# Start addresses of the streamed operands moved off multiples of 64 bytes in a two-mixture float32 block

## The chip, the cores and the metric

The kernel runs on one core of a Trainium2 chip. The time is device microseconds (us) of that core for one execution of the whole program. Durations of single instructions are in nanoseconds (ns).

## The reference, cut to what matters

An attention with a sigmoid in place of a softmax is followed by two dense feed-forward layers, called mixtures here. All arrays are float32.

```
scores = q @ k.T / sqrt(64) - log(448);  attn = sigmoid(scores);  o = attn @ v     # 4 batches x 12 heads x 448 x 64
x = o as [1792 tokens, 768]
h = x @ w_in;  x = (h * cos(h)) @ w_out                                           # 768 -> 2048 -> 768
g = x @ w_gate;  v = x @ w_val;  out = (g * sigmoid(g) * v) @ w_out               # 768 -> 1536 -> 768
```

## The kernel before, in words

Everything is held transposed: features lie on the 128 partitions, tokens along the free dimension, in four groups of 448 tokens. One matmul takes a 128x128 block of weights as the stationary operand and streams 448 columns of tokens past it, as the moving operand.

The precision of float32 is got from pairs. A value is split into a high part `hi` (a copy in float32r, the format that TensorE streams in one pass) and a low part `lo` (the rest, `value - hi`). A product is three matmuls, in the order of `THREE`: hi by hi, hi by lo, lo by hi. Each of them has its own weight load.

The stages:

- Attention, over 24 pairs of heads. Line 655 makes scores, line 667 and line 691 the remainder of 64 keys, line 687 weighs the values, with plain float32 operands. The result is split into the tile of the first mixture's input: hi by ScalarE (line 723), lo by VectorE (line 625).
- The first mixture. Line 1007 multiplies the input `X1` by blocks of `w_in`; ScalarE and VectorE make h*cos(h) from the result and `split_g` writes its hi and lo into one of four activation buffers `g0` to `g3`; line 867 multiplies these by blocks of `w_out`.
- The second mixture. Line 953 makes the gate and the value products by a scheme with seven products of half matrices in place of eight (tokens `1 5 2 6 7 3 4`); their moving operands are seven tiles `X[i]`, made from the sums of the first mixture, hi and lo, in the room of the first input. The activations go through the same four buffers `g0` to `g3` into line 867.

The input tiles `x0` and `x1` hold 43,008 bytes on each partition. `X1` and `X` are views of them, and `rest`, the last part of `x1`, becomes room for weight pairs in the second mixture. Each activation buffer holds hi and lo of 448 tokens, 3,584 bytes on a partition. Every operand in these tiles begins a multiple of 448 elements (1,792 bytes, which is 28 times 64) or of 384 elements (1,536 bytes, 24 times 64) from the tile's start, and each tile starts on a multiple of 64 bytes.

Which instruction comes when on each engine is set by a planner (`Order`) that runs while the program is built, with costs written in the code; a matmul costs `PRODUCT = 0.2025` us there. Nothing in the planner looks at an address. Helper lines 236 and 239 record most ScalarE and VectorE operations, so in the profile these are told apart by their tiles.

Of the kernel before, what the change touches and what calls it, by code (L numbers as in the profile page):

```python
# [10 lines left out]
F32R = mybir.dt.float32r  # L11
# [139 lines left out]
def block_kernel(  # L151
# [12 lines left out]
    P = 128  # L164
# [3 lines left out]
    KD = outT.shape[0] // P  # L168
    T = outT.shape[1]
    N = S  # L170
    KH = KD // 2
    W = KH * P
    NH = T // (2 * N)
# [13 lines left out]
    xp = ctx.enter_context(tc.tile_pool(name="xp", bufs=1))  # L187
# [5 lines left out]
    R = [xp.tile([P, 2, KD, N], F32, tag=f"r{h}", name=f"r{h}") for h in range(NH)]  # L193


    first_x = [xp.tile([P, KD * 2 * 2 * N], F32R, tag=f"x{h}", name=f"x{h}") for h in range(NH)]
    X1 = [x.rearrange("p (k m t) -> p k m t", k=KD, m=2) for x in first_x]
    PLACES = {1: (0, 0), 5: (0, 1), 2: (0, 2), 6: (0, 3), 7: (1, 0), 3: (1, 1), 4: (1, 2)}
    size = KH * 2 * N
# [21 lines left out]
    pairs, singles, gslots, tmps, downbanks = (Slots(order) for _ in range(5))  # L221

    def make_pairs(pool, n, name):
        for i in range(n):
            pairs.give(pool.tile([P, 2, 2, KH, P], F32R, tag=f"w{name}{i}", name=f"w{name}{i}"))
# [217 lines left out]
    def loads():  # L443
        for n, need in enumerate(needs()):
            if n == 2 * NF1 - 4:
                free_t.give((yield convs))
            t = yield free_t
            for w, f, i, k in need:
                there, event = scratch[id(w), f + i]
                yield event  # L450
                there = scratch[id(w), f + i][0]
                if k is None:
                    yield move(t, there)
                else:
                    yield move(t[:, i * W:(i + 1) * W], there[:, k * W:(k + 1) * W])
            arrived = order.event()
            arrivals.append((t, arrived))
            if waiting_load:
                waiting_load.pop(0).set()
            order.spawn(landed(arrived), 0)  # L460
# [101 lines left out]
    def inputs(h):  # L562

        b11, b12, b21, b22 = (R[h][:, j, k * KH:(k + 1) * KH] for k in range(2) for j in range(2))
        make = {
            1: (b11, None), 2: (b21, None), 5: (b11, (b12, b11)), 6: (b11, (b22, b11)),
            7: (b12, (b22, b12)), 4: (b21, (b21, b11)), 3: (b22, None),
        }

        def to_hi(out, t):  # L570
            def do(engine):
                if engine == "ACT":
                    nc.scalar.activation(out=out, in_=t, func=AF.Copy)
                else:
                    nc.vector.tensor_copy(out, t)  # L575
            return {"ACT": 1.55, "DVE": 1.2}, do


        made_t, split_x = ({i: order.event() for i in ORDER} for _ in range(2))
        after = {5: [split_x[1]], 6: [split_x[5]], 7: [made_t[5]], 4: [split_x[2], made_t[6]]}  # L580

        def operand_of(i):
            t, parts = make[i]
            time = due[n_first + h * (NF2 // 2), 0, i]
            if parts:
                for event in after[i]:
                    yield event
                yield by(time - 5.0, vec(1.6, t, parts[0], parts[1], SUB))
                made_t[i].set()
            yield x_left[h - 1, i] if h else x_used[PLACES[i][0]]  # L590
            hi, lo = X[i][:, :, 0], X[i][:, :, 1]
            yield by(time - 3.2, to_hi(hi, t))
            yield by(time - 1.7, vec(1.6, lo, t, f32(hi), SUB))
            split_x[i].set()
            x_ready[h, i].set()

        yield source[h]
        for i in ORDER:
            order.spawn(operand_of(i), 0)
# [419 lines left out]
    def tensor_engine():  # L1019
        turn = itertools.count()  # L1020
        downs = (want for want in ())
        for n in range(n_units):
            if n < n_first:
                for i in range(2):
                    yield from up(n, i, upbanks[next(turn) % 4])
                    for _ in range(between(n)[i]):
                        yield from some(downs)
            else:
                z = {}
                for u in range(2):  # L1030
                    yield from seven(n, u, next(turn), z, downs)
            downs = down(n)
            if n_first - 2 <= n < n_first or n == n_first + NF2 // 2 - 1:
                order.spawn(presets(n), 0)
        while (yield from some(downs)):
            pass

    with tc.manual_schedule():
        nc.gpsimd.memset(nlog, -math.log(S))
        for h in range(NH):  # L1040
            order.spawn(inputs(h), 3.5)
        order.spawn(loads(), 3)
        order.spawn(operands(), 4)
        for raw, t in lent:
            returned.append(order.event())
            order.spawn(conversions(raw, t, returned[-1]), end)
        attention()
        with tc.tile_pool(name="mp", bufs=1) as mp:
            for i in range(2):
                raws.give(mp.tile([P, WT, 2], I32, tag=f"raw{i}", name=f"raw{i}"))  # L1050
                order.spawn(conversions(), end)
            sum_room.append(mp.tile([P, W], F32, tag="sum", name="sum"))
            convs.give(mp.tile([P, WT], F32, tag="cv", name="cv"))
            convs.give(ring[:, 2])
            make_pairs(mp, 3, "b")
            for i in range(4):
                gslots.give(mp.tile([P, 2, N], F32R, tag=f"g{i}", name=f"g{i}"))
            for i in range(3):
                tmps.give(mp.tile([P, 2, N], F32, tag=f"u{i}", name=f"u{i}"))
            order.spawn(tensor_engine(), 0)  # L1060
            order.run()
            assert not order.open
# [51 lines left out]
```

## Time and profile before

| what | value |
|---|---|
| median of the runs shown (lowest, highest) | 1119.46 us (1116.98 to 1119.54) |
| span of the profiled execution, first to last instruction | 1111.8 us |
| median less that span | 7.7 us |
| TensorE matmul busy | 1099.8 us, 99% of the span |
| TensorE share of the chain that ended last | 95% |
| VectorE busy, ScalarE busy, GpSimd busy | 827.0, 578.8, 83.0 us |
| DMA queues, mean rate | 132 GB/s |

The device time of the profiled execution by itself is not listed; its span stands for it, with 7.7 us around it. Matmuls are pipelined: one matmul's record lasts about 365 ns, while the next one starts some 200 ns after it. So the pace is read from how many matmuls lie in a stretch without a gap, and not from the mean duration of one.

### The profile page before, as it was taken

How to read it: one execution, taken by the hardware profiler on the slowest of the kernel's cores; microseconds unless marked ns; L12 is line 12 of the kernel's file. 1: busy time of each engine (PE TensorE's matmuls, PEld its weight loads, DVE VectorE, ACT ScalarE, POOL GpSimd, SP SyncE). 2: the span in 40 equal slices, each digit the busy share in tenths (PEclk: the TensorE clock that was granted, in tenths of full speed). 3: DMA queues.
4: the chain of work that ended last, by engine and by line, in shares of the span. 5: the costliest groups of instructions: out<-in, count | busy, mean ns of one | idle time of the engine just before them, and what ended most of it. 6: DMA issues, size and time to landing. Idle time of an engine off the chain costs nothing.

```text
span 1111.8 us, 14428 instructions
## 1 busy us (share of the span) xinstructions
PE 1099.8 (99%) x5555; PEld 963.7 (87%) x5555; DVE 827.0 (74%) x1193; ACT 578.8 (52%) x868; POOL 83.0 (7%) x70
## 2 busy tenths in 40 slices
PE   9999999999999999999999999999999999999998
PEld 5555579999999999999999889999998999999997
DVE  6888866788788878887778977687779636546644
ACT  5877766644454444454446765444436654333330
POOL 0000000000000000000000321111212101102100
PEclk9999999999999999999999999999999999999999
DMA  7997635544454434443422244434431421121102
GB/s 220 238 252 191 164 114 178 195 153 160 131 178 146 164 117 156 156 146 112 140 101 86 94 148 160 152 128 157 143 128 54 143 88 57 43 72 57 43 1 99
DMA packets 51908, 146.42 MB, mean 132 GB/s; under 512 B 5760, under 2 KB 21120, under 8 KB 51840
## 3 DMA queue, kind: packets, MB, share of 16 engines
q1 hardware_dynamic: 51696, 145.28, 41.1%
q8 instruction: 43, 0.70, 0.3%
q10 hardware_dynamic: 144, 0.23, 0.1%
q14 instruction: 25, 0.20, 0.1%
HBM read 113.25 MB, written 32.24 MB: 131 GB/s over the span
## 4 chain that ended last, share of the span: by engine, by line
PE 95%; DVE 4%; DMA 0%; issue 0%; ACT 0%; ACTq 0%; DVEq 0%
PE banks L867 36%; PE banks L953 26%; PE banks L1007 21%; PE banks L687 5%; PE banks L655 5%; PE banks L691 2%; PE banks L667 1%; DVE x L239 1%; DVE r L239 1%; DVE u L239 1%; DMA r<-in_qk 0%; DVE g L239 0%; DVE wb L239 0%; DVE x L575 0%; ACT r L236 0%
## 5 line engine op out<-in xcount | busy, mean ns | idle before, releaser
L867 PE MATMUL banks<-g,wb 128*128 128x448 f32 x1080 | 240.2, 366 | 0.6 <-DVE g L239 0.6
L867 PEld LDWEIGHTS banks<-g,wb 128*128 128x128 f32 x1080 | 202.8, 188 | 17.5 <-DVE g L239 0.9
L239 DVE TENSOR_TENSOR r<-banks,r 128x896 f32<-128x896 f32 (+1 forms) x133 | 144.0, 1083 | 98.5 <-PE banks L867 97.2
L867 PE MATMUL banks<-g,wa 128*128 128x448 f32 x792 | 179.9, 366 | 1.5 <-DVE g L239 1.5
L867 PEld LDWEIGHTS banks<-g,wa 128*128 128x128 f32 x792 | 148.7, 188 | 13.9 <-DVE g L239 1.9
L953 PE MATMUL banks<-x,wb 128*128 128x448 f32 x702 | 152.2, 366 | 1.4 <-DVE wb L239 0.7
L953 PEld LDWEIGHTS banks<-x,wb 128*128 128x128 f32 x702 | 131.7, 188 | 12.9 <-DVE wb L239 1.1
L1007 PE MATMUL banks<-x,wb 128*128 128x448 f32 x648 | 137.2, 365 | 0.0
L1007 PEld LDWEIGHTS banks<-x,wb 128*128 128x128 f32 x648 | 121.8, 188 | 9.6
L236 ACT ACTIVATE u<-u 128x448 f32<-128x448 f32 x150 | 86.3, 576 | 73.7 <-DVE u L756 40.9
L236 ACT ACTIVATE u<-banks 128x448 f32<-128x448 f32 x104 | 56.3, 541 | 126.2 <-PE banks L1007 88.8
L236 ACT ACTIVATE g<-u 128x448 fp32r<-128x448 f32 x106 | 60.9, 575 | 98.9 <-DVE u L239 84.5
L239 DVE TENSOR_TENSOR u<-u,banks 128x448 f32<-128x448 f32 x124 | 76.2, 615 | 47.3 <-PE banks L953 42.6
L1007 PE MATMUL banks<-x,wa 128*128 128x448 f32 x504 | 106.2, 365 | 0.0
L1007 PEld LDWEIGHTS banks<-x,wa 128*128 128x128 f32 x504 | 94.7, 188 | 7.4
L953 PE MATMUL banks<-x,wa 128*128 128x448 f32 x396 | 86.8, 366 | 0.0
L953 PEld LDWEIGHTS banks<-x,wa 128*128 128x128 f32 x396 | 74.4, 188 | 6.1
L239 DVE TENSOR_TENSOR g<-u,g 128x448 fp32r<-128x448 f32 x106 | 68.4, 648 | 6.0 <-ACT g L236 6.0
L953 PE MATMUL banks<-x,x 128*128 128x448 f32 x315 | 69.8, 367 | 1.8 <-DVE x L239 1.0
L645 ACT ACTIVATE a<-banks,r 128x896 f32<-128x896 f32 x72 | 67.4, 1006 | 7.1 <-PE banks L655 5.2
L756 DVE SCALAR_TENSOR_TENSOR u<-u 128x448 f32<-128x448 f32 x64 | 39.9, 623 | 39.7 <-ACT u L236 39.4
L471 POOL TENSOR_TENSOR sum<-t 128x384 f32<-128x384 f32 x14 | 19.6, 1399 | 644.7 <-DVE t L239 551.0
(105 smaller groups left out, 1362.3 us busy)
## 6 DMA issues: line engine op xcount, KB each, us to landing
raw<-in_w_out SPq DMA_DIRECT2D x24, 768.0 KB, 4.8
r<-in_qk SPq DMA_DIRECT2D x47, 224.0 KB, 6.8
raw<-in_w_in SPq DMA_DIRECT2D x12, 768.0 KB, 4.7
raw<-in_w_gate SPq DMA_DIRECT2D x12, 768.0 KB, 5.0
raw<-in_w_val SPq DMA_DIRECT2D x12, 768.0 KB, 4.6
vs<-in_v SPq DMA_DIRECT2D x24, 320.0 KB, 6.1
t<-swg SPq DMA_DIRECT2D x17, 384.0 KB, 3.5
t<-swi SPq DMA_DIRECT2D x15, 384.0 KB, 3.1
```

The source lines that it names most:

```text
L236: return {"ACT": time}, lambda _: nc.scalar.activation(**kw)
L239: return {"DVE": time}, lambda _: nc.vector.tensor_tensor(out=out, in0=in0, in1=in1, op=op)
L471: on.tensor_tensor(out=out, in0=a, in1=b, op=op)
L645: nc.scalar.activation(out=a, in_=sc, func=AF.Sigmoid, bias=nlog, scale=1.0 / math.sqrt(D))
L655: nc.tensor.matmul(sc[:, j], lhsT=k[half, m, c * P:(c + 1) * P], rhs=q[half, p], start=n == 0, stop=n == 2,)
L667: nc.tensor.matmul(sc, lhsT=blocks[:, m, 0], rhs=q[:, p], start=n == 0, stop=n == 2)
L687: nc.tensor.matmul(o[half], lhsT=vw[:, 2 * c + j], rhs=a[:, j], start=c == 0, stop=False)
L691: nc.tensor.matmul(o, lhsT=blocks[:, m, 1], rhs=b[:, p], start=False, stop=n == 2)
L756: yield {"DVE": 0.65}, lambda _: nc.vector.scalar_tensor_tensor(out=f, in0=f, scalar=MAGIC, in1=u, op0=ALU.subtract, op1=ALU.subtract), ti ...
L867: nc.tensor.matmul(banks[:, first + e - d, :N], lhsT=w[:, m, e % KH if layer == 2 else e, :], rhs=g[:, p], start=(i, m, p) == (0, 0, 0) an ...
L953: nc.tensor.matmul(bank, lhsT=w[:, m, k, :], rhs=x[:, k, p, :], start=(k, m, p) == (0, 0, 0) and i in (1, 5), stop=(k, m) == (KH - 1, 1), ...
L1007: nc.tensor.matmul(out, lhsT=w[:, m, k, :], rhs=x[:, k, p, cols], start=(k, m, p) == (0, 0, 0), stop=(k, m) == (KD - 1, 1),)
```

## The change

Each of the two input tiles and the four activation buffers is allocated 16 elements (64 bytes) larger on each partition, and the part that is used begins a few elements into it: 10 and 6 elements (40 and 24 bytes) for `x0` and `x1`; 4, 8, 12 and 14 elements (16, 32, 48 and 56 bytes) for `g0` to `g3`. The shape of what is used and the order of the instructions on every engine, with what each waits for, are the same. The tiles that are allocated behind these lie up to 384 bytes further on, still on multiples of 64 bytes. The weight pairs that live in the last part of `x1` begin 24 bytes past a multiple of 64. The attention's own operands stay on multiples of 64 bytes.

```
--- before.py
+++ after.py
@@ -193,7 +193,10 @@
-    first_x = [xp.tile([P, KD * 2 * 2 * N], F32R, tag=f"x{h}", name=f"x{h}") for h in range(NH)]
+    def shifted(pool, size, shift, name):
+        return pool.tile([P, size + 16], F32R, tag=name, name=name)[:, shift:shift + size]
+
+    first_x = [shifted(xp, KD * 2 * 2 * N, (10, 6)[h], f"x{h}") for h in range(NH)]
@@ -1054,7 +1057,8 @@
             for i in range(4):
-                gslots.give(mp.tile([P, 2, N], F32R, tag=f"g{i}", name=f"g{i}"))
+                g = shifted(mp, 2 * N, (4, 8, 12, 14)[i], f"g{i}")
+                gslots.give(g.rearrange("p (m n) -> p m n", m=2))
```

## Rows read from the trace of the kernel before

**Rows 1.** The page: span, busy time of TensorE and VectorE, granted clock.

```profile
span 1111.8 us, 14428 instructions
PE 1099.8 (99%) x5555; PEld 963.7 (87%) x5555; DVE 827.0 (74%) x1193; ACT 578.8 (52%) x868; POOL 83.0 (7%) x70
PEclk9999999999999999999999999999999999999999
```

**Rows 2.** The page: the chain that ended last, by engine and line.

```profile
PE 95%; DVE 4%; DMA 0%; issue 0%; ACT 0%; ACTq 0%; DVEq 0%
PE banks L867 36%; PE banks L953 26%; PE banks L1007 21%; PE banks L687 5%; PE banks L655 5%; PE banks L691 2%; PE banks L667 1%; DVE x L239 1%; DVE r L239 1%; DVE u L239 1%; DMA r<-in_qk 0%; DVE g L239 0%; DVE wb L239 0%; DVE x L575 0%; ACT r L236 0%
```

**Rows 3.** All waits of TensorE: releaser, us in total, times, longest.

```profile
PE banks L867 <- DVE g L239: 2.1, 2, 1.5
...
PE banks L953 <- DVE x L239: 1.0, 1, 1.0
PE banks L953 <- DVE u L239: 0.8, 1, 0.8
```

**Rows 4.** TensorE's matmuls by line and operands: count, busy us, mean ns.

```profile
L867 PE MATMUL banks<-g,wb 128*128 128x448 f32 x1080 | 240.2, 366 | 0.6 <-DVE g L239 0.6
L867 PE MATMUL banks<-g,wa 128*128 128x448 f32 x792 | 179.9, 366 | 1.5 <-DVE g L239 1.5
...
L1007 PE MATMUL banks<-x,wb 128*128 128x448 f32 x648 | 137.2, 365 | 0.0
L1007 PE MATMUL banks<-x,wa 128*128 128x448 f32 x504 | 106.2, 365 | 0.0
```

**Rows 5.** Busy time in stretches without a gap on TensorE.

```profile
core 0: us, PE busy (x) PEld busy (x) DVE busy (x) ACT busy (x) POOL busy (x), PEclk, DMA share, GB/s
150.00:600.00 450.00, 450.00 (x2223) 417.24 (x2222) 355.23 (x499) 230.06 (x366) 2.03 (x2) 1.00 0.43 147
...
652.00:731.00 79.00, 79.00 (x384) 71.75 (x383) 58.98 (x76) 41.85 (x64) 14.25 (x11) 1.00 0.45 150
...
853.20:1092.00 238.80, 238.80 (x1180) 221.37 (x1179) 137.89 (x182) 102.70 (x160) 26.06 (x23) 1.00 0.21 63
```

**Rows 6.** The chain in order of time: start us, us, what.

```profile
701.20 3.72 PE banks L953 x18
707.40 5.58 PE banks L953 x27
...
748.09 5.47 PE banks L953 x27
```

**Rows 7.** TensorE in order of time, where the slower pace begins.

```profile
648.26 0.67 PE L953 MATMUL banks<-x,x 128*128 128x448 f32 x2
649.89 1.71 PE L953 MATMUL banks<-x,x 128*128 128x448 f32 x7 [0.95 <-DVE x L239]
```

**Rows 8.** Weight loads of line 687 in order of time, in attention.

```profile
83.95 0.14 PEld L687 LDWEIGHTS banks<-a,vs 128*64 128x64 f32 x2 [0.23 <-issue]
...
85.08 0.14 PEld L687 LDWEIGHTS banks<-a,vs 128*64 128x64 f32 x2 [0.23 <-issue]
```

**Rows 9.** What reads or writes x: duration ns min/median/max, starts.

```profile
L953 PEld LDWEIGHTS banks<-x,wb x702: 186/188/190, 609.5 to 1082.4; 128*128 128x128 f32 x176
L953 PE MATMUL banks<-x,wb x702: 362/365/477, 609.7 to 1082.6; 128*128 128x448 f32 x176
L953 PE MATMUL banks<-x,wa x396: 361/365/370, 688.6 to 1086.8; 128*128 128x448 f32 x198
L953 PE MATMUL banks<-x,x x315: 358/365/475, 611.5 to 1070.4; 128*128 128x448 f32 x158
L867 PE MATMUL banks<-g,x x144: 361/365/370, 740.6 to 1088.1; 128*128 128x448 f32 x144
L953 PE MATMUL banks<-x x99: 362/366/370, 662.0 to 1031.5; 128*128 128x448 f32 x99
L625 DVE TENSOR_TENSOR x<-banks,x x24: 615/617/625, 17.9 to 150.8; 128x448 fp32r<-128x448 f32 x24
L239 DVE TENSOR_TENSOR x<-r,x x14: 1543/1547/2371, 599.2 to 866.8; 128x1344 fp32r<-128x1344 f32 x14
```

**Rows 10.** What reads or writes g, the same columns.

```profile
L236 ACT ACTIVATE g<-u x106: 557/578/589, 159.3 to 1092.6; 128x448 fp32r<-128x448 f32 x106
L239 DVE TENSOR_TENSOR g<-u,g x106: 606/618/1447, 160.0 to 1093.7; 128x448 fp32r<-128x448 f32 x106
```

## The prediction

> **What bounds the kernel now.** I read the busy times first. TensorE's matmuls fill 1099.8 of the span's 1111.8 us, at a clock that the profile shows at its upper level, 2.4 GHz, in every slice [rows 1]. Then the chain that ended last: 95% of it is matmuls, and lines 867, 953 and 1007, the mixtures, hold 83% [rows 2]. The list of waits says how little is left beside that: TensorE's longest waits in the mixtures are 2.1, 1.0 and 0.8 us in total [rows 3]. VectorE is busy for 74% and is waited for in 4% of the chain. So the time is the number of matmuls times their pace, and only a change of pace can move it by much.
>
> How many: lines 867, 953 and 1007. By operands they are 1080 + 792 + 144 on line 867, 702 + 396 + 315 + 99 on line 953 and 648 + 504 on line 1007 [rows 4, 9]: 2016 + 1512 + 1152 = 4680. All of them stream 448 columns, 2664 from x and 2016 from g, so every one has its moving operand shifted. In 558 of them (315 + 99 + 144) the weights too lie in x1's last part.
>
> The pace: in the 450 us from 150 on TensorE has no gap and 2223 matmuls [rows 5], which gives 450/2223 = 202.4 ns (a stretch counts the records that reach over its edges, so the true pace is a little longer); 27 matmuls of line 953 take 5.47 us on the chain [rows 6], 202.6 ns. I use 202.6. At 2.4 GHz and one column a cycle, 448 columns are 186.7 ns. So 15.9 ns of every matmul, 8%, are not columns. That excess is what an address could act on.
>
> Two more things about it stand in the trace. First, plain float32 does not have it to that degree: the matmuls of line 687 come in pairs, and three steps from one pair of weight loads to the next take 85.08 - 83.95 = 1.13 us [rows 8], 377 ns for 448 columns, which is 2.02 cycles a column at 2.4 GHz, or half of it 188.3 ns. The excess belongs to streaming four bytes a column at the full rate. Second, the pace has two values. From 652 to 731 us 384 matmuls fill 79.00 us [rows 5], 205.7 ns by the same rough division, and on the chain 18 take 3.72 us and 27 take 5.58 us, 206.7 ns each, where later the same 27 take 5.47 [rows 6]. The slower stretch begins when TensorE starts again after a wait of 0.95 us [rows 7] and holds for lines 953 and 867 alike. Same instructions, same operands, same clock: the pace depends on how the stream fell into step at its start. So it is not purely a matter of columns, and a change of phase within a line of memory might touch it.
>
> **The change part by part.** It adds no instruction, takes none away, and alters neither the order on any engine nor a wait, a DMA or a queue. No DMA reads or writes x or g. What is left are start addresses.
>
> *The matmuls' moving operand.* Each stream begins 16 to 56 bytes past a multiple of 64 and ends as far past one. No operand of the trace does so, so the price per matmul is bounded from both sides. From above: if data comes in pieces of 64 bytes (16 columns), an aligned row of 448 columns is 28 pieces and a shifted one touches 29; a piece costs 16 cycles at 2.4 GHz, 6.7 ns, or 1/28 of the pace, 7.2 ns. From below: the excess vanishes as far as in plain float32, 202.6 - 188.3 = 14.3 ns less. Between them lies nothing at all: a stream that is read ahead across its pieces does not care where it begins. I take zero. The rows nearest to it are those of the steady pace: it is the same for x and g, at steps from one operand to the next of every kind that the program has, over 450 us, which is what a cost per instruction looks like, and a cost per instruction (the change from one stream to the next) has no address in it. 4680 x 0 = 0 us.
>
> *The stationary operand in x1's last part.* 558 weight loads begin 24 bytes past a multiple of 64. A load takes 188 ns and lies beside the matmul before it [rows 9], within 202.6 ns. If each took one piece of 64 bytes more, 6.7 ns, it would still end inside; without that cover it would be 558 x 6.7 = 3.7 us. I take 0.
>
> *ScalarE and VectorE on the shifted tiles.* The splits into g take 578 and 618 ns, 106 times each [rows 10]; those into x 617 ns 24 times, and 1547 ns 14 times [rows 9]. They walk 448 elements in about 600 ns, far slower than TensorE reads, so a few bytes at either end weigh less. Even 2% on all that the chain shows of them (VectorE on x 1%, on g under half a percent, so at most 17 us [rows 2]) is 0.3 us. I take 0; what hides the rest is TensorE's own work, since TensorE waits only a few us for them [rows 3].
>
> *Tiles pushed further on* stay on multiples of 64 bytes: 0.
>
> The sum is 1111.8 + 0 us of span, and with the 7.7 us around it 1119.5 us, the median of the runs shown. One thing is open in either direction: how many stretches run at the slower pace. The one of before costs about 384 x 4.1 = 1.6 us; none, or two more like it, move the time by -1.6 to +3.2 us. These runs spread over 2.6 us already.
>
> **The rivals.**
>
> *One more piece for each matmul (slower).* If the stream's excess comes from fetching, and pieces are whole, the shift costs 6.7 to 7.2 ns in each of 4680 matmuls: 31 to 34 us, 1151 to 1153 us. For it speaks that plain float32, which asks for half the bytes a second, has almost no excess: the stream is near the limit of something that delivers bytes. Against it: 15.9 ns may as well be paid once per matmul. Smaller pieces give a milder form: with 16 bytes (4 columns) a piece is 202.6 x 4/448 = 1.8 ns, and it strikes only starts that are no multiple of 16, all of x and g3 (2664 + 504 = 3168 matmuls): 5.7 us, 1125 us. A third form is that the stream always falls into the slower step of 206.7 ns: 4296 matmuls x 4.1 = 17.6 us, 1137 us. The rival decides from 0.7 ns a matmul on (3.4 us over 4680). The Trainium skill, page "SBUF — State Buffer", section Specifications, gives lines of 16 bytes and says that each crossing to a new line pays a penalty unless a line is hit at least twice. By that page the shifts of 40, 24 and 56 bytes would make 113 lines of 112, and the milder form above is what it would cost; the trace has only aligned starts and can't say.
>
> *The excess shrinks (faster).* If aligned starts are the bad phase, for example because weights and columns both begin on the same boundary and get in each other's way, then shifting the columns alone frees part of the 15.9 ns. For it speaks that the pace has two values for the same work, so a part of it is a matter of step. A gain as large as the difference of these two, 4.1 ns, would be 19 us, 1100 us; down to plain float32's 188.3 ns it would be 14.3 x 4680 = 67 us, 1053 us, if VectorE kept up (74% now). Against it: the pace is the same however the addresses of two matmuls in a row differ, by thousands of bytes. The Trainium skill, page "TensorE: Matmul & The Clock Gate", section "Wait — 56ns, not 53.3ns?", gives a step of the columns at 2.4 GHz plus about 2.5 ns, 189.2 ns here; the measured 202.6 ns does not agree, and by the page the far end of this rival would be an estimated 63 us.
>
> *A price outside these bounds*, such as two passes for a shifted row, 377 ns a matmul, would add over 800 us; nothing in the trace points there.
>
> **How the numbers follow.** About 0.3% (3.4 us) is what a measurement of this kernel can tell from no change. No change of pace: 0.41. Slower in one of the three forms: 0.31, of which the whole pieces 0.12, the slower step 0.07, small pieces and anything like them 0.11, and 0.01 for a price beyond. The excess shrinks: 0.28, more than half of it by less than 6 ns (1091 us). The predicted time is that of the likeliest, 1119.5 us; its own range is 1116 to 1123. The range over all cases takes in the whole piece, to 1153, and gains to 1091; it leaves out about 0.12 below and 0.03 above.
>
> **What would show it.** If I am right, the chain still shows 27 matmuls of line 953 in 5.47 us (or 5.58 in a stretch), and the 450 us without a gap still hold some 2223. The rival of pieces would show 5.65 to 5.67 us for 27, the milder one 5.52 us on line 953 and 5.47 on line 867 with g0 to g2; the other rival 5.36 or less. Different paces for the matmuls of different buffers would say that the shift itself, and not merely being off a boundary, counts. My forecast is wrong if the steady pace moves at all, since nothing else here is large enough to move the time.

## The result, and the profile after

The changed kernel takes 1122.12 us (median of 18 runs, 1120.66 to 1123.84), the kernel before 1116.28 us in the same company (18 runs, 1110.28 to 1119.54). The ratio is 1.006, with an interval of 1.0044 to 1.0076: slower by 0.6%, inside the range and on the far side of the 0.3% that the forecast called no change.

The page of the changed kernel, the lines that answer to [rows 1] and [rows 2]:

```profile
span 1120.3 us, 14428 instructions
...
PE 1109.2 (99%) x5555; PEld 965.9 (86%) x5555; DVE 826.5 (74%) x1193; ACT 578.7 (52%) x868; POOL 82.7 (7%) x70
...
PEclk9999999999999999999999999999999999999999
...
PE 97%; DVE 2%; DMA 0%; ACT 0%; issue 0%; ACTq 0%; DVEq 0%
```

TensorE's matmuls are busy for 9.4 us more, the other engines for as long as before, and the clock is the same. So the time went into the pace of the matmuls. The stretch from 150 to 600 us without a gap, to be held against the first row of [rows 5]:

```profile
150.00:600.00 450.00, 450.00 (x2199) 413.14 (x2198) 350.74 (x494) 226.58 (x361) 2.04 (x2) 1.00 0.43 147
```

2199 matmuls where there were 2223: 1.1% fewer. The chain in order of time (start us, us, what) shows that there is no longer one pace:

```profile
296.51 3.71 PE banks L1010 x18
300.22 4.96 PE banks L870 x24
305.18 3.72 PE banks L1010 x18
308.90 2.44 PE banks L870 x12
...
705.52 3.71 PE banks L956 x18
...
711.68 5.54 PE banks L956 x27
717.21 2.48 PE banks L870 x12
...
732.00 5.61 PE banks L956 x27
```

(Lines 1010, 870 and 956 are 1007, 867 and 953 of the kernel before.) 27 matmuls of line 956 take 5.54 us here and 5.61 there, 205 to 208 ns a matmul, where [rows 6] had 5.47 or 5.58; 12 of line 870 take 2.44 or 2.48 us, 203 to 207 ns. The views leave out buffer numbers; told apart by the order in which the program uses the buffers, the means from start to start of the records from 150 us on are 203.4 ns for g0, 203.9 for g1, 204.6 for g2, 205.0 for g3, 205.3 for x0 and 206.3 for x1. Over all mixture matmuls it is 205.08 ns, where the profiled execution of before has 203.00 (202.67 outside its slower stretch). The difference, 2.08 ns over some 4660 matmuls, is 9.7 us; TensorE's waits are 1.0 us shorter; the two spans differ by 8.5 us.

What VectorE and ScalarE do on the shifted tiles lasts as long as before. Duration min/median/max of two such operations in the changed kernel:

```profile
L628 DVE TENSOR_TENSOR x<-banks,x x24: 616/619/626, 17.9 to 150.8; 128x448 fp32r<-128x448 f32 x24
L956 PE MATMUL banks<-x,wb x702: 362/368/473, 614.6 to 1091.1; 128*128 128x448 f32 x176
```

VectorE's split into x went from 617 to 619 ns, against [rows 9]; the matmul's record is 3 ns longer.

### The profile page after: what moved, and what is told of

Read it like the earlier page. It is cut to its first block, busy times and chain, and to the rows that moved or that the text cites. A ratio compares the mean times of both kernels' runs of the same rounds, so it can differ in the third digit from the quotient of the medians.

```text
span 1120.3 us, 14428 instructions
## 1 busy us (share of the span) xinstructions
PE 1109.2 (99%) x5555; PEld 965.9 (86%) x5555; DVE 826.5 (74%) x1193; ACT 578.7 (52%) x868; POOL 82.7 (7%) x70
## 4 chain that ended last, share of the span: by engine, by line
PE 97%; DVE 2%; DMA 0%; ACT 0%; issue 0%; ACTq 0%; DVEq 0%
PE banks L870 36%; PE banks L956 27%; PE banks L1010 21%; PE banks L690 5%; PE banks L658 5%; PE banks L694 2%; PE banks L670 1%; DVE r L242 0%; DVE x L242 0%; DMA r<-in_qk 0%; DVE u L242 0%; DVE g L242 0%; DVE wb L242 0%; ACT banks L239 0%; ACT r L239 0%
## 5 line engine op out<-in xcount | busy, mean ns | idle before, releaser
L956 PE MATMUL banks<-x,wb 128*128 128x448 f32 x702 | 154.2, 368 | 0.8 <-ACT banks L239 0.7
L1010 PE MATMUL banks<-x,wb 128*128 128x448 f32 x648 | 138.8, 367 | 0.0
L1010 PE MATMUL banks<-x,wa 128*128 128x448 f32 x504 | 107.7, 367 | 0.0
L956 PE MATMUL banks<-x,wa 128*128 128x448 f32 x396 | 87.9, 368 | 0.0
```

The lines of the kernel that those rows point to most:

```text
L956: nc.tensor.matmul(bank, lhsT=w[:, m, k, :], rhs=x[:, k, p, :], start=(k, m, p) == (0, 0, 0) and i in (1, 5), stop=(k, m) == (KH - 1, 1), ...
L1010: nc.tensor.matmul(out, lhsT=w[:, m, k, :], rhs=x[:, k, p, cols], start=(k, m, p) == (0, 0, 0), stop=(k, m) == (KD - 1, 1),)
```

## The experiments

Three theories were open once the pace was seen to differ by buffer: A, a stream that begins off a boundary touches one more piece of memory; B, columns and weights fall into step with each other, and the difference of their two starts decides in which; C, only going from a tile of one start to a tile of another costs.

**The stream by itself.** A kernel that only streams 448 columns past a block of weights, 60 matmuls to a group; the tile names give the starts in bytes past a common base (x for columns, w for weights). It leaves out the whole reference.

```
SEGMENTS = [(o, 0, 448) for o in [0, 0, 0, 0] + list(range(8, 256, 8)) + [0, 0, 0, 0]]
SEGMENTS += [(o, w, 448) for o in (0, 40) for w in (8, 16, 24, 32, 40, 48, 56)]
SEGMENTS += [(0, 0, n) for n in (512, 384, 320, 256)]
for s, (o, w, n) in enumerate(SEGMENTS):
    ...
    for i in range(RUN):
        nc.tensor.matmul(bank[:, :n], lhsT=wt, rhs=x[:, a:a + n], start=True, stop=True)
```

> This kernel computes nothing of the reference: it streams 448 columns of float32r past 128x128 weights, 60 matmuls for each start address, with a wait on VectorE between the groups, and writes zeros as its output. Starts of the columns go from 0 to 248 bytes in steps of 8 with the weights on a multiple of 64; then the weights' start is moved; then the number of columns. Theory A (pieces): the pace depends on the columns' start alone; with pieces of 16 bytes 202.6 ns on every multiple of 16 and 204.4 ns on odd multiples of 8, with pieces of 64 bytes 209 ns on every start that is no multiple of 64; the weights' start does nothing. Theory B (step): the matmul's excess of 16 ns is a wait for a step between two streams, columns and weights; the pace then depends on the difference of both starts, lies on a few values such as 200, 202.7 and 206.7 ns, and the same starts can give two of them in different groups. Theory C (mixture): every start has the same pace by itself, 202.7 or 206.7, and what the change costs comes from going between tiles of different starts; then all groups here show only these two paces. With the number of columns: an excess that is paid once a matmul stays at 16 to 20 ns for 256 to 512 columns; one that is paid by the byte goes from 9 to 18 ns.

TensorE in order of time (start us, us):

```profile
40.00 12.65 PE L46 MATMUL banks<-x0b,w0b 128*128 128x448 f32 x60 [0.38 <-DVE w0b L43]
53.04 12.43 PE L46 MATMUL banks<-x0b,w0b 128*128 128x448 f32 x60 [0.38 <-DVE w0b L43]
65.85 12.46 PE L46 MATMUL banks<-x8b,w0b 128*128 128x448 f32 x60 [0.38 <-DVE w0b L43]
78.70 12.28 PE L46 MATMUL banks<-x16b,w0b 128*128 128x448 f32 x60 [0.39 <-DVE w0b L43]
91.36 12.65 PE L46 MATMUL banks<-x24b,w0b 128*128 128x448 f32 x60 [0.39 <-DVE w0b L43]
...
479.39 12.66 PE L46 MATMUL banks<-x0b,w0b 128*128 128x448 f32 x60 [0.38 <-DVE w0b L43]
492.43 12.42 PE L46 MATMUL banks<-x0b,w0b 128*128 128x448 f32 x60 [0.38 <-DVE w0b L43]
...
634.57 13.03 PE L46 MATMUL banks<-x40b,w24b 128*128 128x448 f32 x60 [0.39 <-DVE w24b L43]
647.98 12.46 PE L46 MATMUL banks<-x40b,w32b 128*128 128x448 f32 x60 [0.38 <-DVE w32b L43]
...
699.60 13.89 PE L46 MATMUL banks<-x0b,w0b 128*128 128x512 f32 x60 [0.38 <-DVE w0b L43]
713.88 10.67 PE L46 MATMUL banks<-x0b,w0b 128*128 128x384 f32 x60 [0.38 <-DVE w0b L43]
724.94 9.07 PE L46 MATMUL banks<-x0b,w0b 128*128 128x320 f32 x60 [0.38 <-DVE w0b L43]
734.39 7.45 PE L46 MATMUL banks<-x0b,w0b 128*128 128x256 f32 x60 [0.38 <-DVE w0b L43]
```

A group lasts 59 steps and, for the first weight load and the last matmul, some 0.47 us with 448 columns: 12.28 us is 200 ns a matmul, 12.43 is 202.7, 12.65 is 206.5, 13.03 is 213. Equal starts give 202.67 and 206.67 in turn, the very two values of the kernel before, with nothing else around. Other starts give other paces, and moving the weights with the columns where they are (40 bytes, weights 24 or 32) changes it from 213.3 to 203.3 ns. Of the starts that are multiples of 64, 64 bytes gives 200.0, 128 gives 204.0 and 192 gives 202.2. Theory A, a pace by the columns' start alone, falls, and so does C, which allowed two paces only. Theory B holds in that both starts count, but their difference alone does not fix the pace: 16 bytes of difference give 200.0 ns with the weights at 0 (12.28 us) and 213.3 with the columns at 40 and the weights at 24 (13.03 us). The excess over one column a cycle has a floor that is paid once a matmul: start to start 226.67, 173.33, 146.67 and 120.0 ns for 512, 384, 320 and 256 columns, 13.3 ns more than the columns in each case. What varies comes on top of this floor, which is 200.0 ns for 448 columns. At these four lengths equal starts lie on the floor; at 448 columns they lie 2.7 or 6.7 ns above it. So what the starts do was measured for 448 columns alone.

**Larger rooms without a shift; the inputs alone; the activations alone.** The changed kernel with shifts (0, 0) and (0, 0, 0, 0); with (10, 6) and (0, 0, 0, 0); with (0, 0) and (4, 8, 12, 14).

```
-    first_x = [shifted(xp, KD * 2 * 2 * N, (10, 6)[h], f"x{h}") for h in range(NH)]
+    first_x = [shifted(xp, KD * 2 * 2 * N, (0, 0)[h], f"x{h}") for h in range(NH)]
...
-                g = shifted(mp, 2 * N, (4, 8, 12, 14)[i], f"g{i}")
+                g = shifted(mp, 2 * N, (0, 0, 0, 0)[i], f"g{i}")
```

> The rooms are 16 elements larger, as in the changed kernel, but every shift is 0. All three theories: no different from before, 1116 us within the spread of its runs (1110 to 1120), with the paces 202.7 and 206.7 ns. If it is slower by 6 us as the changed kernel is, the cause is where the tiles behind lie (weights on multiples of 256 and not 128 past them), and not the shift.

> Only the input tiles are shifted (10 and 6), the activation buffers are not. In the changed kernel's trace the matmuls on x were 2.7 and 3.7 ns slower than 202.6, those on g 0.8 to 2.4. Theory A: x pays 2664 x 1.8 = 4.8 us and g nothing, 202.6 ns on every g. Theory B: x keeps 205 to 206, g is free to take any step after x, between 200 and 207. Theory C: most of the cost stays, since nearly every change of tile is between x and g: 4 to 6 us above a before at 202.7.

> Only the activation buffers are shifted (4, 8, 12, 14), the input tiles are not. Theory A: 504 x 1.8 = 0.9 us, since only the fourth buffer starts off a multiple of 16; x at 202.6 ns. Theory B: g keeps 203 to 205, x falls into 202.7 or 206.7 by how the stream reaches it. Theory C: as much as with x alone.

Rooms alone: 1112.25 us, ratio 0.9989 (0.997 to 1.0008), no different. Inputs alone: 1118.95 us, 1.004 (1.0021 to 1.0059). Activations alone: 1116.1 us, 1.0012 (0.9988 to 1.0035). The rooms are the steadier thing to hold the two others against (1111.09 to 1113.90 us in 12 runs): the inputs add 6.7 us to them and the activations 3.9 us (1114.89 to 1116.97, no run in common). So most of the cost comes with the inputs, and a part with the activations.

But the sum of the rooms hides something: with no shift at all the buffers already have paces of their own, 204.7 ns for g0, 200.8 for g1, 203.8 for x0 and 202.3 for x1 (start to start, weights in their own tiles). The larger rooms had moved the tiles against each other by 64 bytes at a time, and the gains and losses cancel. Every step inside these tiles, and inside the weights' tiles, is a multiple of 256 bytes, so a tile's columns always start equally far past the weights modulo 256, that is, in what is left over by whole 256s. By the sizes of the tiles in order of allocation that is 0 bytes for g0, 64 for g1, 128 for x0 and 192 for x1 here; the stream test has 202.67 or 206.67, 200.0, 204.0 and 202.2 ns for these starts. That the tiles stay on multiples of 64 is no protection.

The distance is not all, though. x0 and x1 are streamed 18 matmuls at a time, and in the first mixture they keep these paces when the activations are shifted (204.0 and 202.4 ns). g0 and g1 take turns after every three matmuls; with the inputs alone shifted, g1 stands 64 bytes past the weights as in the rooms kernel, and has 202.9 ns in the first mixture where it has 199.9 there. Nothing but the inputs' place differs in that stage, so what is streamed in between enters too.

**Whether the wait before a group decides, and whether the weights' bytes do.** The stream kernel again: eleven starts, six groups of 40 each after waits of different length, then narrower weights. It too leaves out the reference.

```
STARTS = (0, 16, 32, 40, 48, 64, 96, 128, 160, 192, 208)
SEGMENTS = [(o, 448, P, 1 + 37 * r) for o in STARTS for r in range(6)]
SEGMENTS += [(0, n, P, 1 + 37 * r) for n in (384, 512) for r in range(4)]
SEGMENTS += [(o, 448, m, 1 + 37 * r) for m in (64, 32) for o in (0, 40) for r in range(2)]
```

> Computes nothing of the reference, as the first of this kind. Eleven starts of the columns, each in six groups of 40 matmuls that begin after waits of different length; the weights stay on their place. Then 384 and 512 columns, and weights of 64 and 32 columns. Theory B (step): each start has its own few paces and the length of the wait decides among them; starts 16, 64 and 160 bytes ahead of the weights give 200.0 ns in most groups, 0 gives 202.7 and 206.7 in turn, 40 and 208 stay above 203. Fewer columns of weights mean less to fetch beside the stream, so the excess of 13 to 20 ns should fall: about a half with 64, a quarter with 32, and the differences between starts with it. If the excess is instead paid once for each matmul whatever the weights (a change from one stream to the next), it stays at 13 to 20 ns with 64 and 32 too. A pace by the start alone (theory A) would give one pace for each start, whatever the wait.

```profile
24.43 8.38 PE L47 MATMUL banks<-x0b,w0b 128*128 128x448 f32 x40 [0.51 <-DVE w0b L44]
33.35 8.37 PE L47 MATMUL banks<-x0b,w0b 128*128 128x448 f32 x40 [0.55 <-DVE w0b L44]
42.32 8.53 PE L47 MATMUL banks<-x0b,w0b 128*128 128x448 f32 x40 [0.59 <-DVE w0b L44]
...
274.45 8.27 PE L47 MATMUL banks<-x64b,w0b 128*128 128x448 f32 x40 [0.44 <-DVE w0b L44]
283.20 8.28 PE L47 MATMUL banks<-x64b,w0b 128*128 128x448 f32 x40 [0.48 <-DVE w0b L44]
...
327.32 8.48 PE L47 MATMUL banks<-x96b,w0b 128*128 128x448 f32 x40 [0.44 <-DVE w0b L44]
336.27 8.48 PE L47 MATMUL banks<-x96b,w0b 128*128 128x448 f32 x40 [0.48 <-DVE w0b L44]
...
665.62 8.31 PE L47 MATMUL banks<-x0b,w0b 128*64 128x448 f32 x40 [0.44 <-DVE w0b L44]
```

Each difference of starts has one pace or a few. 64 bytes ends at 200.0 ns in six groups of six, 96 at 205.33, 128 and 208 at 204.0, 40 at 204.45, 192 at 202.2; 16 ends at 200.0 or 202.2, 0 at 202.67 or 206.67 and 32 at 200, 204.4 or 206.67. That the length of the wait picks among them is not shown: each group also writes to another of four banks, and in the first stream test the groups of equal starts alternate between the two paces after waits of 0.38 or 0.39 us. Narrower weights do not lower the excess to a half or a quarter: with 64 and with 32 columns of weights equal starts give 202.2 ns, 15.5 ns over the columns, and 40 bytes gives 201.7 to 206.7. That part of the expectation was wrong; the cost does not follow the weights' bytes.

**One difference for all.** All six tiles shifted alike, in rooms 64 elements larger, so that every tile keeps its place within 256 bytes: 16, 32 and 10 elements.

```
-        return pool.tile([P, size + 16], F32R, tag=name, name=name)[:, shift:shift + size]
+        return pool.tile([P, size + 64], F32R, tag=name, name=name)[:, shift:shift + size]
-    first_x = [shifted(xp, KD * 2 * 2 * N, (10, 6)[h], f"x{h}") for h in range(NH)]
+    first_x = [shifted(xp, KD * 2 * 2 * N, 16, f"x{h}") for h in range(NH)]
-                g = shifted(mp, 2 * N, (4, 8, 12, 14)[i], f"g{i}")
+                g = shifted(mp, 2 * N, 16, f"g{i}")
```

> All six tiles shifted by 16 elements (64 bytes), rooms 64 elements larger so that every tile still begins where it does before within 256 bytes; columns then start 64 bytes ahead of the weights. In the stream of one start this difference gave 200.0 ns in six groups of six. Theory B: 200.0 ns on every x and g except where the weights lie in x1 itself, 4680 x 2.67 = 12 us less than a run of before at 202.67 throughout (about 1110), so 1098 us, and no spread over the runs. Theory A (multiples of 64 or 16 bytes cost nothing, the rest something): the same as before, 1110 to 1120.

> The same with 32 elements (128 bytes). Theory B: 204.0 ns, as in all six groups with this start: 4680 x 1.33 = 6 us more than a run at 202.67 throughout, 1116 us, with little spread over the runs. Theory A: as before, since 128 is a multiple of 64.

> The same with 10 elements (40 bytes) for all six tiles, the shift that the first input tile has in the changed kernel. Theory B: 204.45 ns, 8 us more than a run at 202.67 throughout, 1118 us. Theory A: 204.4 ns for all with pieces of 16 bytes, 1118 to 1119 too (this run tells B from A only together with the other two); with pieces of 64 bytes 209 ns, 1140 us. Theory C (only the change from tile to tile costs): no cost, 1110 to 1120.

With 64 bytes: 1102.71 us, 0.9883 of the kernel before (0.9861 to 0.9905), and 200.0 to 200.1 ns on every x and g whose weights lie in their own tiles; the 1098 us expected had counted all 4680 matmuls at 200.0. With 128 bytes: 1116.26 us, 1.0 (0.9979 to 1.002), 203.9 ns. With 40 bytes: 1111.19 us, 0.9963 (0.9947 to 0.998). Busy time in the same stretch of the 64- and the 128-byte kernel (us, matmuls, clock):

```profile
160.00:600.00 440.00, 440.00 (x2202) 1.00 0.43 147
```

```profile
160.00:600.00 440.00, 440.00 (x2158) 1.00 0.43 145
```

2202 against 2158 matmuls in 440 us, with all starts of both kernels on multiples of 64. And 40 bytes, off such a multiple, is no slower than before. Its chain in order of time:

```profile
302.86 3.60 PE banks L1010 x18
306.46 2.43 PE banks L870 x12
308.89 3.60 PE banks L1010 x18
```

The expectation of 1118 us for 40 bytes missed: in the kernel the stream of line 1010 settles at 200.0 ns with it, and x has 201.5 ns on average (weights in their own tiles), where the stream test had 204.45 in all six groups. So the test's paces carry over only for some starts. The test kept one block of weights and two places of columns where the kernel goes through many; whether that is the reason was not tested.

**The weights that lie in the input tile; the weights moved in place of the columns.** First, on top of the 64-byte kernel, the pairs in x1's last part 48 elements (192 bytes) further on. Second, on the kernel before, all weight pairs 192 bytes further on and nothing else: the same change of `rest`, and the second cut.

```
-    rest = first_x[1][:, 3 * size:]
+    rest = first_x[1][:, 3 * size + 48:]
```

```
-            pairs.give(pool.tile([P, 2, 2, KH, P], F32R, tag=f"w{name}{i}", name=f"w{name}{i}"))
+            w = pool.tile([P, 4 * KH * P + 64], F32R, tag=f"w{name}{i}", name=f"w{name}{i}")
+            pairs.give(w[:, 48:48 + 4 * KH * P].rearrange("p (m a k c) -> p m a k c", m=2, a=2, k=KH))
```

> As the kernel with all six tiles 64 bytes on, with one thing more: the weight pairs in the last part of the second input tile begin 192 bytes further on, so that there too the columns start 64 bytes ahead of the weights (modulo 256). In the run before, the matmuls with these weights took 204.2 to 206.7 ns and all others 200.0. Theory B: these fall to 200 as well, some 550 x 5 ns = 2.7 us less, 1100 us. If the place of the weights inside that tile does nothing: 1102.7 us as before.

> The activations and inputs stay where they were in the kernel before; all weight pairs begin 192 bytes further on instead, so that the columns again start 64 bytes ahead of the weights modulo 256. If the difference of the two starts alone sets the pace: 200.0 ns on all, 1100 us. If the place of each stream by itself matters too (in the first stream test, moving the weights by 16, 32 and 48 bytes did not give the pace of moving the columns back by as much), another pace: between 200 and 207 ns, 1100 to 1133 us. Theory A, the columns' start alone: as before, 1110 to 1120.

1099.71 us and 1100.66 us, both 0.9848 of the kernel before (0.9832 to 0.9864 and 0.9828 to 0.9868). The chain of the second one, in order of time:

```profile
693.14 3.60 PE banks L954 x18
696.74 2.40 PE banks L868 x12
699.14 5.40 PE banks L954 x27
```

18 in 3.60, 12 in 2.40 and 27 in 5.40 us: 200 ns everywhere, in this kernel (line 954 is 953 of the kernel before) and in the first of the two. Columns 64 bytes past the weights modulo 256, with this one distance for all matmuls, give the same pace whichever of the two was moved. These two are the fastest versions here.

## Why the prediction came out as it did

The time fell inside the range by luck. By its own sign, "wrong if the steady pace moves at all", the forecast failed: the pace moved by 2.08 ns a matmul, and the span grew by 8.5 us that the sum had at zero. The sum came near all the same, because it began some 5.9 us too high (see the time around the span, below).

*What bounds the kernel* held: the pace of 4680 matmuls is the time, and TensorE's waits moved by 1.0 us only. VectorE and ScalarE on shifted tiles cost nothing, as taken.

*The step that failed* is the price of the moving operand, taken as zero because "a cost per instruction (the change from one stream to the next) has no address in it". Part of that fits: no steady stream went under 13.3 ns of excess, whatever the starts, and that much was paid with 256 to 512 columns alike. The rest, 2.7 or 6.7 ns in the kernel before, does have an address in it: it changes with where columns and weights start against each other. The steady pace over 450 us that I leaned on says nothing against this, since by the tiles' sizes the kernel before keeps that distance at 0 modulo 256 for every matmul. The prediction had the clue, two paces for the same work, and said that a change of phase might touch it, and then priced it at nothing. It measured 2.08 ns a matmul between the two profiles, 9.7 us; in the changed kernel the distances are 168 and 216 bytes for x, 16, 96, 176 and 248 for g (modulo 256, weights in their own tiles), six different ones. The stream test has 206.0 and 205.0 ns for the first two and 200.0 or 202.2, 205.3, 204.4 and 205.1 for the others; the kernel's 205.3 and 206.3, 203.4, 203.9, 204.6 and 205.0 have the same size, but differ from these by up to 3.4 ns. So that the shift costs is shown, by the rooms without it; how much it costs does not follow from the table of distances.

*The weights in x1's last part*, taken as hidden beside the matmul: their loads last as long as before (188 to 189 ns), but their start changes the pace of the 558 matmuls that use them. With the columns at 64 bytes, putting these weights right was worth 3.0 us, 1102.71 to 1099.71.

*Tiles pushed further on*, taken as zero since they stay on multiples of 64: zero in the sum (0.9989, interval over 1), not in the parts (200.8 to 204.7 ns by tile).

*The time around the span* was mis-sized: 7.7 us was the median of some runs less the span of another. Spans and times of one run lie 1.8 us apart (1120.3 and 1122.11). The profiled execution of before was thus one of about 1113.6 us, 5.9 less than the sum began with; 1113.6 and the 8.5 us by which the span grew are the 1122.1 measured. That the runs of before spread over 1110 to 1126 us, and those of the 64-byte kernels over some 3 us, fits its two paces: the 2304 matmuls of the first mixture at 206.67 in place of 202.67 are 9.2 us. No trace of one of the longer runs was taken, so this is argued from the stream test's groups.

*The rivals.* One more piece for each matmul falls in all forms, though its milder form had the size, 5.7 us where the medians differ by 5.8. That is luck: it left g0 to g2 at the old pace, and they have 203.4 to 204.6 ns; and 128 bytes, a multiple of every piece considered, is slower than 64 and than 40, and moving the weights alone brings the whole gain. The Trainium skill's lines of 16 bytes (page "SBUF — State Buffer", section "Specifications (TRN2)") do not decide the pace here: starts of 64 and 128 bytes both lie on such lines and differ by 4.0 ns. The third form, 206.7 ns throughout, is not what the buffers show. The faster rival named what matters, the starts of columns and weights against each other, and its price for it, some 1100 us, was reached with one distance of 64 bytes. Its condition holds only in part: equal starts are not the worst, 96 and 128 bytes are slower than 202.67 (205.3 and 204.0).

*What stays open*: which resource the two streams share, why equal distances give different paces in different surroundings, and what picks the pace after a pause. Neither the weights' width nor the columns' number changes the extra in proportion, so it is not simply bytes; and the pace for a given distance was measured, not derived.

## What to carry to other kernels

Where TensorE's pace sets the time and the operands are float32r, read the pace from counts in stretches without a gap, and compare it with the columns at the granted clock: if the rest is above 13 ns a matmul, the place of columns against weights within 256 bytes is worth a sweep in the kernel itself, with one distance for all matmuls. The test of a single stream gave the kernel's pace for 64 and for 128 bytes and missed it for 40. Being on a multiple of 64 bytes, or off it, says nothing by itself. A pace that changes after a wait, with the same instructions and clock, is the sign to look for, and any edit that resizes a tile can move it.

## What the runs showed of the hardware that was not expected

A float32r matmul of 256 to 512 columns, each with its own weight load, took at least 13.3 ns more than one column a cycle at 2.4 GHz (120.0 ns for 256, 226.67 for 512). The Trainium skill, page "TensorE: Matmul & The Clock Gate", section "Wait — 56ns, not 53.3ns?", gives about 2.5 ns for back-to-back matmuls; the measurement differs here.

Two streams of the same instructions hold different paces for as long as nothing interrupts them (202.67 and 206.67 ns with equal starts, 200.0, 204.4 and 206.67 with 32 bytes between them). A pause can change the pace, and in the kernel before the slower one ended at 731 us with two longer steps, of 230 and 276 ns, and no listed wait. The slowest that was seen in a steady stream was 213.3 ns, with the columns at 40 bytes and the weights at 24.
